# First keys and values by a casting software load, all phi loads from SyncE, and a new order of steps in an attention and expert kernel

## The chip, the cores and the metric

The kernel runs on one core of one Trainium2 chip. The metric is the device time of one execution in microseconds, as the median of repeated runs. The profile beside it shows one execution: the span from the first to the last instruction of the program, and the busy time of the engines in it. The engines are TensorE (PE, with its weight loads as PEld), VectorE (DVE), ScalarE (ACT), GpSimd (POOL) and SyncE (SP). Transfers run on 16 DMA engines; GpSimd issues them on a queue that the profile calls software_dynamic, SyncE and ScalarE on queues called hardware_dynamic.

## The reference

There are 8 batches of 8 heads, 576 positions and a head size of 64. Each head's keys and values are first condensed into 32 memory slots with the weights `softmax(phi)`; the queries then attend to the slots. The result, as 4608 rows of 512, goes through a dense two-layer network and through one of eight experts per row, chosen by the largest gate; the two results are added.

```python
# phi: (8, 8, 576, 32); q, k, v: (8, 8, 576, 64)
a = softmax(phi, axis=2)                      # over the positions
k_m = einsum('bhsm,bhsd->bhmd', a, k)
v_m = einsum('bhsm,bhsd->bhmd', a, v)
x = softmax(q @ k_m.T / sqrt(64)) @ v_m       # then to rows (4608, 512)

y = relu(x @ w1_dense) @ w2_dense
e = argmax(x @ w_gate, axis=1)                # one expert per row
y += softmax(x @ w_gate)[e] * (relu(x @ w1[e]) @ w2[e])
```

(The code above is shortened; the reference is written out with numpy, with small constants added to the sums.)

## The kernel before

The program works on one batch at a time, but the steps of neighbouring batches are interleaved. Every step has a short name and a batch number, and one long text gives the order in which all steps are emitted. Each engine carries out its own instructions strictly in that order, so an instruction that waits holds everything behind it on its engine. A letter behind a step's slash names the engine (A is ScalarE, V VectorE, P GpSimd).

The steps of a batch, in the order of their dependence: `Lphi`, `Lq`, `Lk`, `Lv` load the inputs; `e0`, `e1` take the exponential of phi (ScalarE); `z` and `kv` are the sums and the key-value product (TensorE); `kvm`, `T`, `kTc`, `vTc` scale and transpose it; `q0`, `q1`, `qT0`, `qT1` transpose the queries; `s`, `ET`, `Z`, `ln`, `inv`, `A` are the second softmax; `vg`, `pc`, `choose` find the batch's expert; `w1`, `w2` load that expert's matrices (GpSimd must first read the expert's number); `L`, `mxeq`, `ex`, `gates` are the gates of the rows; `fd`, `vd`, `hd`, `Hd` are the dense hidden layer; `fe`, `ve`, `he`, `He` the expert's; `yd` and `ye` add both second layers into one output bank, chunk by chunk; `Y` copies it to the y tile and `o` stores it.

The order begins so:

```python
ORDER = """
stage3:0 Lq:0 ciota:0 cones:0 stage1:0 Lphi1:0 Lwg:0 wgt:0 Lphi0:0 stage4:0 cast1:0/V cast3:0/P
cid:0 cblk:0 cast4:0/V warm:0/8 stage0:0 stage5:0 warm:0/8 e0:0 warm:0/8 wgm:0 e1:0 wgc:0 cast5:0/A
ciotac:0 cast0:0/P stage2:0 z:0 Lphi:1 q0:0 q1:0 qT0:0/A Lw1d:0 cast2:0/A qT1:0/A kv:0 rz:0 kvm:0
# ... (cut: Lphi:2/A, Lphi:3/A, Lphi:4/A, Lphi:5, Lphi:6/A, Lphi:7 come later, each near its own batch)
```

The loads. The tiles of q, k and v are f16 and the inputs f32, so GpSimd's transfers cast on the way. The exception is batch 0, whose k and v come in six f32 pieces through SyncE and are cast by the engines:

```python
inp = ctx.enter_context(tc.tile_pool(name="inp", bufs=3))      # phi, q, kv: three batches each
big = ...(bufs=2, PSUM); one = ...(bufs=3, PSUM); sml = ...(bufs=1, PSUM)
NKEEP = 4                                                      # y tiles

@step("Lphi")
def _(b, i, e):
    input_tile(b, "phi")
    (nc.scalar if e == "A" else nc.sync).dma_start(
        out=st[b]["phi"].rearrange("p h t m -> p h (t m)"),
        in_=phi[b].rearrange("h (p t) m -> p h (t m)", t=T),
    )

@step("Lv", "Lk")
def _(b, i, e):
    src, u = (v, 1) if i == "Lv" else (k, 0)
    input_tile(b, "kv")
    nc.gpsimd.dma_start(out=st[b]["kv"][:, u]..., in_=src[b]...)   # f32 -> f16
# ... (cut: Lq in the same way; Lphi0 and Lphi1 load the two halves of phi of batch 0)

pieces = [(0, 1, 0, 3, 0), (1, 0, 0, 3, 0), (0, 1, 3, 3, 3), (1, 0, 3, 3, 3), (2, 1, 6, 2, 0), (2, 0, 6, 2, 2)]

@step(*(f"stage{i}" for i in range(len(pieces))))
def _(b, i, e):
    n_tile, u, h0, n, at = pieces[i]
    # ... the stage tiles share the buffers of y:
    # wk.tile([P, 6, T, Dh], F32, tag="y", name="stage", bufs=NKEEP)
    nc.sync.dma_start(out=st[b]["stage", n_tile][:, at : at + n]..., in_=(k, v)[u][b, h0 : h0 + n]...)
```

The output. A chunk of 128 rows leaves PSUM for a y tile, of which there are four, and is stored by SyncE. A fifth batch can write its y only when one of the four has been stored:

```python
@step(*(f"Y{c}" for c in range(NCH)))
def _(b, c, e):
    if "y" not in x:
        x["y"] = wk.tile([128, S * D // 128], F32, tag="y", name="y", bufs=NKEEP)
    # ... ScalarE or VectorE copies p_y to y

@step(*(f"o{c}" for c in range(NCH)))
def _(b, c, e):
    # ... nc.sync.dma_start(out=dst, in_=y[...])
```

Of the kernel before, what the change touches and what calls it, by code (L numbers as in the profile page):

```python
# [24 lines left out]
ex:0 mxeq:0 gates:0 hd3:0 Hd2:0/A hd0:0 Hd3:0/A Lw2d:0 e0:1 pg:0 z:1 rz:1 kv:1 kvm:1 T:1 Hd0:0/A
hd1:0 vTc:1/V vg:1 Hd1:0/A w2:0 fe:0 ve0:0/A vgc:1 ve1:0/V Lq:2 he1:0 Lk:2 pc:1 gB:0/A fd:1 He1:0
kTc:1/A he2:0 He2:0 vd0:1/A Lphi:2/A he0:0 yd2:0 s0:1 He0:0 ET0:1 he3:0 s1:1 yd1:0 He3:0 Z0:1 ET1:1
vd1:1/V Z1:1 ln0:1 ye2:0 inv0:1 ye1:0 ln1:1 Y1:0/V A0:1 yd4:0 ye4:0 inv1:1 yd3:0 q1:2 choose:1 A1:1
Y4:0/A Lv:2 yd0:0 L:1 qT1:2/V e0:2 hd1:1 w1:1 Hd1:1/V ex:1 hd0:1 Hd0:1/A mxeq:1 ye3:0 hd3:1 e1:2
ye0:0 Y0:0/A q0:2 gates:1 Hd3:1/V z:2 Y2:0/A rz:2 kv:2 qT0:2/V hd2:1 kvm:2 pg:1 T:2 Y3:0/A fe:1  # L30
Hd2:1/A gB:1/A w2:1 yd1:1 ve1:1/A vTc:2/V ve0:1/V fd:2 he0:1 vd0:2/A he3:1 Lq:3 vg:2 He0:1 He3:1
vd1:2/A yd4:1 he2:1 Lphi:3/A He2:1 he1:1 kTc:2/A He1:1 yd0:1 s1:2 vgc:2 Lv:3 ye4:1 Lk:3 s0:2 ET1:2
Y4:1/V pc:2 Z1:2 ye0:1 choose:2 ET0:2 ln1:2 Z0:2 Y0:1/V ln0:2 inv1:2 inv0:2 q0:3 w1:2 yd3:1 A1:2
ye1:1 yd2:1 qT0:3/A e0:3 A0:2 L:2 Lq:4 e1:3 mxeq:2 q1:3 hd2:2 ex:2 ye2:1 qT1:3/V Y1:1/A w2:2 gates:2
hd3:2 z:3 Hd2:2/A rz:3 kv:3 Hd3:2/A pg:2 kvm:3 Y2:1/A hd0:2 gB:2/A T:3 Hd0:2/V fe:2 ve1:2/V ye3:1
hd1:2 Lv:4 ve0:2/A he2:2 vTc:3/V Hd1:2/A fd:3 vg:3 He2:2 he0:2 He0:2 vd1:3/A he3:2 Y3:1/A He3:2
yd0:2 Lphi:4/A he1:2 yd3:2 kTc:3/V s0:3 He1:2 vd0:3/V vgc:3 s1:3 ye3:2 ET1:3 Z1:3 ET0:3 ln1:3 Lk:4
pc:3 ye0:2 Y3:2/V inv1:3 Z0:3 yd1:2 q1:4 ln0:3 q0:4 inv0:3 yd2:2 choose:3 A1:3 A0:3 qT1:4/V ye1:2
qT0:4/A hd1:3 e1:4 e0:4 Y0:2/V L:3 mxeq:3 hd2:3 ex:3 yd4:2 gates:3 Y1:2/A w1:3 ye4:2 ye2:2 z:4
Hd2:3/A Hd1:3/A hd3:3 w2:3 o0:2 rz:4 pg:3 Y2:2/A kv:4 Hd3:3/V Y4:2/A Lq:5 fe:3 Lphi:5 kvm:4 gB:3/A  # L40
hd0:3 ve0:3/A Hd0:3/A T:4 ve1:3/V kTc:4/V he3:3 vTc:4/V He3:3 s1:4 ET1:4 vg:4 fd:4 vgc:4 s0:4 pc:4
ET0:4 choose:4 he0:3 he2:3 He0:3 yd2:3 He2:3 e1:5 vd1:4/A he1:3 vd0:4/A Z0:4 yd0:3 ln0:4 Z1:4 He1:3
inv0:4 ln1:4 inv1:4 A0:4 ye0:3 e0:5 ye2:3 q0:5 qT0:5/A Lk:5 q1:5 Y0:3/V yd3:3 Lv:5 A1:4 ye3:3 L:4
yd4:3 ye4:3 Y3:3/A Y4:3/A ex:4 qT1:5/V hd0:4 mxeq:4 gates:4 hd3:4 yd1:3 w1:4 z:5 Hd0:4/A Hd3:4/V
ye1:3 w2:4 Y2:3/A hd2:4 pg:4 gB:4/V fe:4 Y1:3/A rz:5 kv:5 hd1:4 Hd2:4/A ve0:4/A kvm:5 Hd1:4/V T:5
ve1:4/A kTc:5/A vTc:5/A he3:4 he0:4 vg:5 He3:4 fd:5 s0:5 He0:4 vgc:5 yd1:4 vd0:5/V he2:4 vd1:5/A
ET0:5 pc:5 Lq:6 s1:5 yd2:4 He2:4 ET1:5 choose:5 he1:4 He1:4 Lk:6 Z0:5 Lphi:6/A yd0:4 ln0:5 o4:3
inv0:5 Lv:6 Z1:5 ln1:5 o3:2 A0:5 inv1:5 ye1:4 o1:2 q0:6 o2:2 A1:5 qT0:6/V ye2:4 q1:6 qT1:6/A ye0:4
o4:2 Y2:4/V hd0:5 e0:6 e1:6 hd2:5 Y0:4/V L:5 yd3:4 yd4:4 mxeq:5 ex:5 Lphi:7 ye4:4 gates:5 w1:5
Y1:4/A w2:5 z:6 Hd0:5/A kv:6 Hd2:5/A rz:6 Y4:4/V kvm:6 hd1:5 Hd1:5/V pg:5 T:6 kTc:6/A s0:6 gB:5/V  # L50
s1:6 Lq:7 fe:5 ET0:6 vTc:6/V vg:6 ET1:6 ve1:5/V Lv:7 ve0:5/A hd3:5 ye3:4 he2:5 Hd3:5/A vgc:6 he1:5
pc:6 Y3:4/V e0:7 o3:0 He2:5 o2:0 yd2:5 he0:5 He1:5 Z0:6 yd1:5 o4:0 He0:5 ln0:6 he3:5 Z1:6 yd0:5 o0:0
Lk:7 inv0:6 choose:6 He3:5 A0:6 ye0:5 ln1:6 inv1:6 ye1:5 o1:0 ye2:5 A1:6 L:6 q0:7 e1:7 Y0:5/A Y1:5/V
fd:6 q1:7 Y2:5/A yd3:5 vd0:6/V yd4:5 mxeq:6 qT0:7/A vd1:6/A ex:6 hd1:6 gates:6 ye4:5 qT1:7/A w1:6
Hd1:6/A hd2:6 z:7 pg:6 kv:7 Hd2:6/A rz:7 hd3:6 gB:6/A kvm:7 Y4:5/A Hd3:6/V T:7 o4:5 kTc:7/A hd0:6
s1:7 vTc:7/A Hd0:6/A fe:6 o2:3 o3:3 ye3:5 ve1:6/V vg:7 vgc:7 s0:7 ve0:6/A ET1:7 ET0:7 fd:7 o4:1 o0:3
pc:7 he0:6 Y3:5/V vd1:7/A Z1:7 yd0:6 He0:6 o2:1 ln1:7 he2:6 choose:7 He2:6 vd0:7/A inv1:7 he1:6
He1:6 yd1:6 he3:6 o1:3 Z0:7 ln0:7 He3:6 inv0:7 w2:6 yd3:6 A1:7 A0:7 o3:1 ye3:6 ye1:6 o0:5 Y3:6/A
o2:5 Y1:6/A L:7 yd2:6 yd4:6 ye4:6 hd0:7 o4:4 w1:7 hd3:7 Y4:6/V ye2:6 ex:7 o3:5 o1:1 o0:4 Hd0:7/A
hd2:7 Hd3:7/A Y2:6/A mxeq:7 Hd2:7/A o4:6 w2:7 hd1:7 gates:7 fe:7 o1:4 Hd1:7/V ve0:7/V pn:0 o2:4  # L60
# [7 lines left out]
def kernel(  # L68
# [46 lines left out]
    def copy(e, out, in_):  # L115
        (nc.scalar.copy if e == "A" else nc.vector.tensor_copy)(out=out, in_=in_)  # L116
# [78 lines left out]
    pieces = [(0, 1, 0, 3, 0), (1, 0, 0, 3, 0), (0, 1, 3, 3, 3), (1, 0, 3, 3, 3), (2, 1, 6, 2, 0), (2, 0, 6, 2, 2)]

    @step(*(f"stage{i}" for i in range(len(pieces))))
    def _(b, i, e):
        n_tile, u, h0, n, at = pieces[i]
        input_tile(b, "kv")  # L200
        if ("stage", n_tile) not in st[b]:
            st[b]["stage", n_tile] = wk.tile([P, 6, T, Dh], F32, tag="y", name="stage", bufs=NKEEP)
        nc.sync.dma_start(  # L203
            out=st[b]["stage", n_tile][:, at : at + n].rearrange("p h t d -> p h (t d)"),
            in_=(k, v)[u][b, h0 : h0 + n].rearrange("h (p t) d -> p h (t d)", t=T),
        )

    @step(*(f"cast{i}" for i in range(len(pieces))))
    def _(b, i, e):
        n_tile, u, h0, n, at = pieces[i]  # L210
        s = st[b]["stage", n_tile][:, at : at + n]
        o = st[b]["kv"][:, u, h0 : h0 + n]
        if e == "P":
            nc.gpsimd.tensor_copy(out=o, in_=s)
        else:
            copy(e, out=o, in_=s)
# [664 lines left out]
```

## Time and profile before

| what | value |
|---|---|
| time, median of 3 runs | 185.63 us (185.1 to 185.78) |
| span of the profiled execution | 184.1 us |
| PE busy | 150.3 us (82%) |
| DVE busy | 95.0 us (52%) |
| ACT busy | 99.3 us (54%) |
| POOL busy | 33.7 us (18%) |
| moved by the software queue | 22.42 MB, as f16 |
| moved by the two hardware queues | 14.11 and 2.43 MB |

The busy time of an engine is the time in which it had at least one instruction under way. Where the profile says that an engine was idle before an instruction, it also names what released that instruction: another engine's instruction, or a DMA. "Issue" is time in which it waited for nothing that the profile shows. The share of DMA can pass 1, as packets of one DMA engine overlap. In this profile the largest entry among ScalarE's waits is 25.5 us in 5 waits for phi, and in SyncE's most of its time is spent waiting for finished y tiles.

### The profile page before, as it was taken

To read this page: it belongs to the slowest core of one execution; us is meant where nothing else is said; L and a number is where in the kernel's file an instruction comes from. 1 tells how busy PE (TensorE), PEld (TensorE's weight loads), DVE (VectorE), ACT (ScalarE), POOL (GpSimd) and SP (SyncE) were. 2 spreads that over 40 slices of the span, in tenths; PEclk is the share of its full clock that TensorE was granted. 3 is DMA by queue.
4 is the path that set the end of the run, shared out by engine and by line. 5 is a ranking of instruction groups with operands and counts; after the bars stand their busy time and mean duration, and the time that the engine had idled before them with its cause. 6 is when DMAs were issued, how large, how long until landed. Compare 5 with 4: busy or idle time off the path is not lost.

```text
span 184.1 us, 4484 instructions
## 1 busy us (share of the span) xinstructions
PE 150.3 (82%) x1857; PEld 92.6 (50%) x1857; DVE 95.0 (52%) x256; ACT 99.3 (54%) x167; POOL 33.7 (18%) x49
## 2 busy tenths in 40 slices
PE   5015469789999998999964999991889999999990
PEld 5015337445665565566532665561646564565540
DVE  0073029264786565866761467670538546836610
ACT  2023686557384766389717665622473787647030
POOL 2305309000430260017043000340000300300000
PEclk9999999999999999999999999998559999999998
DMA  5999999999999999999999999999995594999994
GB/s 161 214 250 226 191 201 200 205 205 231 185 191 184 232 213 204 206 237 139 227 229 203 206 205 279 240 305 276 212 204 81 78 151 131 330 168 244 390 367 135
DMA packets 40594, 39.30 MB, mean 213 GB/s; under 512 B 1652, under 2 KB 36468, under 8 KB 40568
## 3 DMA queue, kind: packets, MB, share of 16 engines
q0 software_dynamic: 26752, 22.42, 78.1%
q1 hardware_dynamic: 10600, 14.11, 25.7%
q10 hardware_dynamic: 3216, 2.43, 5.0%
q8 instruction: 16, 0.26, 0.5%
q14 instruction: 10, 0.08, 0.1%
HBM read 51.92 MB, written 9.44 MB: 333 GB/s over the span
## 4 chain that ended last, share of the span: by engine, by line
PE 41%; DMA 40%; ACT 9%; SPq 4%; issue 2%; DVE 1%; ACTq 0%
PE p_y L703 18%; DMA out_dram<-y 17%; DMA phi<-in_phi_dram 12%; PE p_h L629 10%; DMA stage<-in_k_dram 7%; DMA w1e<-in_moe_w_dram 4%; PE p_kv L357 3%; PE p_q L413 2%; ACT E L323 2%; PE p_vw L616 2%; PE p_z L456 2%; PE p_s L432 2%; ACT qT L116 1%; SPq L203 1%; ACT lnz L478 1%
## 5 line engine op out<-in xcount | busy, mean ns | idle before, releaser
L703 PE MATMUL p_y<-w2d,HTd 128*128 128x512 f16 (+1 forms) x192 | 37.5, 346 | 4.0 <-ACT vwd L116 3.8
L703 PE MATMUL p_y<-w2e,HTe 128*128 128x512 f16 (+1 forms) x192 | 37.4, 349 | 0.0
L683 DVE SCALAR_TENSOR_TENSOR HTe<-p_h,gB 128x576 f16<-128x576 f32 x32 | 23.3, 753 | 8.9 <-PE p_h L629 5.8
L237 POOL DMA_DIRECT2D w1e<-in_moe_w_dram x8 | 6.1, 761 | 113.8 <-DVE HTe L683 63.9
L323 ACT ACTIVATE E<-phi 96x768 f16<-96x768 f32 x16 | 13.0, 834 | 25.6 <-DMA phi<-in_phi_dram 25.5
L703 PEld LDWEIGHTS <-HTd 128*128 128x128 f16 (+1 forms) x192 | 14.4, 101 | 16.7 <-issue 7.4
L629 PE MATMUL p_h<-A,vwd 128*128 128x288 f16 x128 | 21.9, 307 | 0.4 <-ACT qT L116 0.4
L703 PEld LDWEIGHTS <-HTe 128*128 128x128 f16 (+1 forms) x192 | 15.4, 103 | 13.1 <-issue 1.7
L629 PE MATMUL p_h<-A,vwe 128*128 128x288 f16 x128 | 19.9, 287 | 0.9 <-ACT vwe L116 0.8
L727 ACT ACTIVATE y<-p_y 128x512 f32<-128x512 f32 (+1 forms) x26 | 14.0, 554 | 12.2 <-PE p_y L703 6.4
L670 ACT ACTIVATE HTd<-p_h 128x576 f16<-128x576 f32 x23 | 14.5, 649 | 9.6 <-PE p_h L629 8.1
L483 DVE TENSOR_TENSOR A<-ET,lnz 128x576 f16<-128x576 f16 x16 | 11.9, 753 | 9.7 <-ACT lnz L478 9.7
L445 ACT ACTIVATE ET<-p_s 128x576 f16<-128x576 f32 x16 | 10.1, 651 | 10.3 <-PE p_s L432 10.3
L629 PEld LDWEIGHTS <-vwe 128*128 128x128 f16 x128 | 11.8, 98 | 7.7 <-issue 1.5
L729 DVE TENSOR_SCALAR y<-p_y 128x512 f32<-128x512 f32 (+1 forms) x14 | 8.8, 630 | 13.1 <-PE p_y L703 12.4
L629 PEld LDWEIGHTS <-vwd 128*128 128x128 f16 x128 | 11.9, 103 | 6.5 <-issue 1.2
L469 ACT ACTIVATE lnz<-p_z 128x576 f32<-128x576 f32 x16 | 10.3, 645 | 7.2 <-PE p_z L456 7.1
L413 PE MATMUL p_q<-ident,q 96*128 96x96 f16 x192 | 12.0, 224 | 1.0 <-DMA q<-in_q_dram 1.0
L413 PEld LDWEIGHTS <-q 96*128 96x128 f16 x192 | 10.8, 108 | 3.2 <-DMA q<-in_q_dram 1.6
L478 ACT ACTIVATE lnz<-lnz 128x576 f32<-128x576 f32 x16 | 10.8, 682 | 0.4
L116 ACT COPY qT<-p_q 128x1152 f16<-128x1152 f16 x9 | 10.0, 1115 | 1.7 <-PE p_q L413 1.7
L357 PE MATMUL p_kv<-kv,E 96*32 96x128 f16 x384 | 8.3, 242 | 2.8 <-ACT kv L116 2.3
(88 smaller groups left out, 180.7 us busy)
## 6 DMA issues: line engine op xcount, KB each, us to landing
out_dram<-y SPq DMA_DIRECT2D x32, 256.0 KB, 4.4
q<-in_q_dram POOLq DMA_DIRECT2D x8, 576.0 KB, 13.0
w1e<-in_moe_w_dram POOLq DMA_DIRECT2D x8, 512.0 KB, 7.6
w2e<-in_moe_w_dram POOLq DMA_DIRECT2D x8, 512.0 KB, 11.4
kv<-in_v_dram POOLq DMA_DIRECT2D x7, 576.0 KB, 18.1
kv<-in_k_dram POOLq DMA_DIRECT2D x7, 576.0 KB, 17.9
phi<-in_phi_dram ACTq DMA_DIRECT2D x4, 576.0 KB, 10.9
phi<-in_phi_dram SPq DMA_DIRECT2D x3, 576.0 KB, 13.0
```

What stands on the lines that cost most here:

```text
L116: (nc.scalar.copy if e == "A" else nc.vector.tensor_copy)(out=out, in_=in_)
L323: nc.scalar.activation(out=x["E"][:, :, a].rearrange("p t j m -> p j t m"), in_=x["phi"].rearrange("p (j a) t m -> p a j t m", a=2)[:, a], ...
L357: nc.tensor.matmul(p_kv[M * j : M * j + M, a], lhsT=x["E"][:, t, a, j], rhs=x["kv"][:, :, 2 * j + a, t], start=(t == 0), stop=(t == T - 1),)
L413: nc.tensor.transpose(p_q[:, j // 2, c : c + P], q8[:, 2 * j + a, 2 * t : 2 * t + 2].rearrange("p t d -> p (t d)"), ident,)
L469: nc.scalar.activation(out=st[b]["lnz"][:, a].rearrange("p (h c) -> p h c", h=2), in_=st[b].pop(("pz", a))[:, :, 0:HC], func=AF.Ln,)
L478: nc.scalar.activation(out=lnz, in_=lnz, func=AF.Exp, scale=-1.0)
L483: eng.tensor_mul(out=A[b][:, a], in0=st[b]["ET"][:, a], in1=st[b]["lnz"][:, a])
L629: nc.tensor.matmul(p_h[:, h, 0:HC], lhsT=vw[:, g, 128 * ft : 128 * ft + 128], rhs=a[:, g, HC * h : HC * h + HC], start=(g == 0), stop=(g = ...
L670: nc.scalar.activation(out=o, in_=p_h, func=AF.Relu)
L683: nc.vector.scalar_tensor_tensor(out=x["HTe"][:, ft].rearrange("p (h c) -> p h c", h=2), in0=x.pop(("pe", ft))[:, :, 0:HC], scalar=0.0, in ...
L703: nc.tensor.matmul(p_y[n * u : n * u + n, 0:w], lhsT=HT[:, ft, lo : lo + n], rhs=w2[:, ft, w * u : w * u + w], start=(half == 0 and ft == ...
L727: nc.scalar.activation(out=o, in_=p_y, func=AF.Copy, scale=1.0 / SC)
```

## The change

The f32 pieces and their casts are gone: k and v of batch 0 now come like those of all other batches, by a casting transfer that GpSimd issues. Phi is loaded by SyncE alone. The order of all steps, loads and stores is new; its purpose is to fit the steps to the new start, and to have inputs there when they are due. The work that is computed is the same.

```diff
 ORDER = """
-stage3:0 Lq:0 ciota:0 cones:0 stage1:0 Lphi1:0 Lwg:0 wgt:0 Lphi0:0 stage4:0 cast1:0/V cast3:0/P
-cid:0 cblk:0 cast4:0/V warm:0/8 stage0:0 stage5:0 warm:0/8 e0:0 warm:0/8 wgm:0 e1:0 wgc:0 cast5:0/A
-ciotac:0 cast0:0/P stage2:0 z:0 Lphi:1 q0:0 q1:0 qT0:0/A Lw1d:0 cast2:0/A qT1:0/A kv:0 rz:0 kvm:0
 ... (cut)
+Lv:0 cones:0 Lq:0 cblk:0 Lphi0:0 Lphi:1 e0:0 Lphi1:0 Lk:0 Lwg:0 wgt:0 cid:0 warm:0/8 warm:0/8 Lphi:2
+wgm:0 wgc:0 e0:1 q1:0 e1:0 qT1:0/V z:0 rz:0 kv:0 kvm:0 q0:0 Lw1d:0 T:0 kTc:0/V vTc:0/V s1:0 e1:1
 ... (cut)
-    pieces = [(0, 1, 0, 3, 0), (1, 0, 0, 3, 0), (0, 1, 3, 3, 3), (1, 0, 3, 3, 3), (2, 1, 6, 2, 0), (2, 0, 6, 2, 2)]
-
-    @step(*(f"stage{i}" for i in range(len(pieces))))
-    def _(b, i, e):
 ... (cut: the staging loads)
-    @step(*(f"cast{i}" for i in range(len(pieces))))
-    def _(b, i, e):
 ... (cut: the casts)
```

What the new order makes of the queues:

```text
SyncE:  first half of phi 0, phi 1, second half of phi 0, gate weights, phi 2,
        store o2 of batch 0, phi 4, phi 3, phi 5, phi 6,
        stores o3 of batch 3, o0 of 0, o1 and o2 of 3, o3, o1, o4 of 0, o4 of 2, o0 and o4 of 3,
        phi 7, then the other stores
GpSimd: v0, q0, k0, w1 dense, q1, k1, v1, | w1 of batch 0's expert, w2 dense, q2, w2 of the expert, v2, k2,
        | w1 of batch 1's, q3, w2, k3, v3, | w1 of 2's, q4, w2, v4, k4, | w1 of 3's, w2, k5, q5, k6, v5,
        | w1 of 4's, v6, q6, w2, | w1 of 5's, q7, w2, k7, v7, | w1 and w2 of 6's, | w1 and w2 of 7's
        (a bar is where GpSimd waits to read the number of a chosen expert)
```

More of the change, by code (lines that the diff above doesn't have):

```diff
@@ L19 @@
 ORDER = """
-stage3:0 Lq:0 ciota:0 cones:0 stage1:0 Lphi1:0 Lwg:0 wgt:0 Lphi0:0 stage4:0 cast1:0/V cast3:0/P
-cid:0 cblk:0 cast4:0/V warm:0/8 stage0:0 stage5:0 warm:0/8 e0:0 warm:0/8 wgm:0 e1:0 wgc:0 cast5:0/A
-ciotac:0 cast0:0/P stage2:0 z:0 Lphi:1 q0:0 q1:0 qT0:0/A Lw1d:0 cast2:0/A qT1:0/A kv:0 rz:0 kvm:0
-T:0 kTc:0/A Lq:1 s1:0 ET1:0 Lv:1 s0:0 vTc:0/V vg:0 ET0:0 Z1:0 Z0:0 ln1:0 vgc:0 inv1:0 pc:0 ln0:0
-inv0:0 fd:0 choose:0 e1:1 Lk:1 vd1:0/A q0:1 A0:0 A1:0 q1:1 L:0 vd0:0/V w1:0 qT0:1/A qT1:1/V hd2:0
@@ L25 @@
[L25 to L60, printed above, removed]
@@ L61 @@
-ve1:7/A pg:7 ye0:6 gB:7/A he2:7 He2:7 Y0:6/A he0:7 He0:7 yd2:7 he1:7 he3:7 o0:1 He1:7 yd0:7 o1:6
-o1:5 yd3:7 He3:7 ye2:7 flags:0 o0:6 o2:6 o3:6 Y2:7/A ye3:7 yd1:7 Y3:7/A ye1:7 o2:7 Y1:7/V ye0:7
-Y0:7/A o3:7 yd4:7 o3:4 ye4:7 o1:7 Y4:7/A o0:7 o4:7/A
+Lv:0 cones:0 Lq:0 cblk:0 Lphi0:0 Lphi:1 e0:0 Lphi1:0 Lk:0 Lwg:0 wgt:0 cid:0 warm:0/8 warm:0/8 Lphi:2
+wgm:0 wgc:0 e0:1 q1:0 e1:0 qT1:0/V z:0 rz:0 kv:0 kvm:0 q0:0 Lw1d:0 T:0 kTc:0/V vTc:0/V s1:0 e1:1
+vg:0 qT0:0/A ET1:0 s0:0 Z1:0 ciota:0 vgc:0 ET0:0 ciotac:0 Lq:1 ln1:0 pc:0 choose:0 inv1:0 Z0:0 fd:0
@@ new lines @@
+ln0:0 q1:1 Lk:1 A1:0 vd1:0/A inv0:0 Lv:1 vd0:0/V q0:1 w1:0 qT0:1/A A0:0 qT1:1/V L:0 mxeq:0 ex:0
+hd0:0 hd3:0 Hd3:0/A z:1 hd1:0 rz:1 kv:1 gates:0 kvm:1 Hd0:0/A Lw2d:0 hd2:0 Hd1:0/A T:1 Hd2:0/V e0:2
+pg:0 kTc:1/V gB:0/A fe:0 vTc:1/A ve0:0/A s0:1 vg:1 ve1:0/V s1:1 vgc:1 ET0:1 Lq:2 fd:1 w2:0 ET1:1
+pc:1 he3:0 he1:0 yd0:0 He3:0 e1:2 He1:0 vd0:1/V Z1:1 vd1:1/A he0:0 yd2:0 He0:0 choose:1 he2:0 ln1:1
+He2:0 yd3:0 Z0:1 q1:2 qT1:2/V inv1:1 ye2:0 ln0:1 ye3:0 Lv:2 inv0:1 Y2:0/A A1:1 yd4:0 q0:2 A0:1 o2:0
+L:1 mxeq:1 hd0:1 Lphi:4 ye4:0 qT0:2/A ex:1 Y3:0/A ye0:0 z:2 Y4:0/A rz:2 Lphi:3 yd1:0 Lk:2 hd2:1
@@ new lines @@
+gates:1 kv:2 Hd0:1/A Hd2:1/A hd1:1 w1:1 hd3:1 kvm:2 T:2 ye1:0 Hd3:1/V Y0:0/V kTc:2/A vTc:2/A pg:1
+Hd1:1/A vg:2 s1:2 gB:1/V fe:1 ET1:2 ve0:1/V ve1:1/A s0:2 vgc:2 Y1:0/V ET0:2 Lq:3 pc:2 he0:1 e1:4
+fd:2 He0:1 he3:1 He3:1 yd2:1 w2:1 vd1:2/A vd0:2/A Z1:2 ln1:2 he2:1 yd3:1 He2:1 Z0:2 he1:1 He1:1
+ln0:2 inv1:2 yd0:1 A1:2 inv0:2 q0:3 ye0:1 A0:2 choose:2 ye2:1 Y2:1/V qT0:3/A q1:3 Y0:1/V Lk:3 L:2
+qT1:3/A ye3:1 yd1:1 hd3:2 hd1:2 Lphi:5 mxeq:2 ex:2 yd4:1 Hd3:2/A e1:3 e0:3 ye4:1 ye1:1 Y3:1/V
+Hd1:2/V Lv:3 gates:2 hd0:2 w1:2 hd2:2 z:3 Hd2:2/A kv:3 rz:3 kvm:3 pg:2 Y4:1/A Lq:4 T:3 w2:2 Y1:1/A
@@ new lines @@
+Hd0:2/A gB:2/V fe:2 kTc:3/A ve0:2/A ve1:2/V s0:3 Lphi:6 s1:3 ET1:3 yd1:2 vTc:3/A he0:2 fd:3 ET0:3
+Lv:4 vd1:3/A vg:3 He0:2 vgc:3 he3:2 Z1:3 ln1:3 He3:2 vd0:3/A pc:3 yd3:2 Lk:4 he2:2 he1:2 e0:4 yd0:2
+inv1:3 He2:2 q0:4 He1:2 Z0:3 ye3:2 choose:3 ln0:3 ye0:2 q1:4 w1:3 A1:3 inv0:3 w2:3 Y0:2/A ye1:2 A0:3
+yd4:2 qT1:4/V qT0:4/A Y3:2/V Y1:2/A L:3 hd1:3 ex:3 yd2:2 mxeq:3 hd0:3 e1:6 ye2:2 gates:3 Hd1:3/A z:4
+kv:4 Hd0:3/V hd3:3 pg:3 rz:4 Y2:2/A kvm:4 Hd3:3/V fe:3 ye4:2 gB:3/A ve0:3/A T:4 Y4:2/A hd2:3 Lk:5
@@ new lines @@
+ve1:3/V he1:3 kTc:4/V vTc:4/V vg:4 fd:4 Hd2:3/A s0:4 He1:3 vd1:4/A vgc:4 yd4:3 vd0:4/V ET0:4 e0:5
+he3:3 He3:3 yd2:3 he2:3 pc:4 he0:3 He2:3 yd1:3 He0:3 Z0:4 ye4:3 e1:5 Lq:5 s1:4 ln0:4 ET1:4 Lk:6
+ye2:3 choose:4 Z1:4 inv0:4 ye1:3 Y4:3/V Y2:3/V A0:4 ln1:4 q0:5 inv1:4 q1:5 A1:4 yd0:3 Y1:3/A qT1:5/V
+Lv:5 L:4 mxeq:4 ye0:3 w1:4 hd1:4 e0:6 ex:4 yd3:3 Lv:6 qT0:5/A gates:4 z:5 Hd1:4/V kv:5 pg:4 rz:5
+Y0:3/A gB:4/A kvm:5 hd0:4 T:5 fe:4 Hd0:4/V kTc:5/A vTc:5/V s1:5 ve1:4/V s0:5 ye3:3 ET1:5 ve0:4/V
+Z1:5 vg:5 ET0:5 ln1:5 hd2:4 vgc:5 Hd2:4/A Y3:3/A inv1:5 hd3:4 fd:5 o3:3 Hd3:4/V he0:4 Lq:6 pc:5
@@ new lines @@
+He0:4 Z0:5 kv:6 ln0:5 w2:4 vd0:5/A he2:4 vd1:5/A he3:4 yd0:4 A1:5 He2:4 he1:4 o0:0 yd1:4 He3:4 o1:3
+o2:3 inv0:5 A0:5 He1:4 L:5 choose:5 mxeq:5 o3:0 q1:6 ye1:4 ex:5 q0:6 z:6 rz:6 ye0:4 w1:5 kvm:6
+qT0:6/A T:6 yd4:4 ye4:4 o1:0 qT1:6/A o4:0 kTc:6/V Y1:4/V s0:6 Y0:4/V gates:5 s1:6 ET1:6 yd2:4 Y4:4/V
+yd3:4 hd3:5 o4:2 ET0:6 hd2:5 Hd3:5/A Hd2:5/A ye2:4 vTc:6/V Z1:6 hd1:5 ln1:6 inv1:6 vg:6 Lq:7 Y2:4/V
+Hd1:5/V o0:3 vgc:6 fe:5 ve1:5/A hd0:5 o4:3 ve0:5/V Z0:6 pc:6 ln0:6 ye3:4 Hd0:5/V inv0:6 w2:5 pg:5
+he2:5 Lk:7 yd3:5 Lphi:7 A1:6 gB:5/A Y3:4/A e0:7 He2:5 e1:7 he0:5 he1:5 yd0:5 A0:6 L:6 He0:5 He1:5
@@ new lines @@
+he3:5 He3:5 ex:6 Lv:7 choose:6 yd1:5 q0:7 q1:7 ye3:5 ye1:5 mxeq:6 ye0:5 z:7 Y1:5/A qT1:7/V gates:6
+Y3:5/A pg:6 Y0:5/V fd:6 gB:6/A yd2:5 ye2:5 w1:6 vd0:6/A rz:7 vd1:6/V qT0:7/A hd2:6 o0:5 hd0:6 Y2:5/A
+kv:7 yd4:5 Hd0:6/A w2:6 Hd2:6/V kvm:7 ye4:5 T:7 Y4:5/A o1:2 fe:6 o0:2 vTc:7/V hd3:6 hd1:6 ve1:6/V
+ve0:6/A o2:2 Hd3:6/A fd:7 Hd1:6/V vg:7 vgc:7 he3:6 vd0:7/A He3:6 he1:6 He1:6 yd3:6 o2:1 he0:6 he2:6
+o4:4 o0:4 kTc:7/A vd1:7/A He0:6 pc:7 yd4:6 choose:7 s0:7 yd0:6 w1:7 ET0:7 He2:6 s1:7 o3:2 ye4:6 o3:5
@@ new lines @@
+Z0:7 o4:5 ET1:7 ye0:6 ln0:7 inv0:7 Y4:6/V Z1:7 ln1:7 Y0:6/V yd2:6 A0:7 w2:7 inv1:7 ye2:6 A1:7 yd1:6
+Y2:6/V L:7 hd3:7 ex:7 hd0:7 ye3:6 o2:5 mxeq:7 Hd3:7/A Hd0:7/A o0:1 o2:6 Y3:6/A hd2:7 Hd2:7/A hd1:7
+o3:4 gates:7 Hd1:7/V fe:7 pn:0 pg:7 ve1:7/A ye1:6 ve0:7/V he1:7 gB:7/A o4:6 He1:7 he3:7 o3:1 yd1:7
+o4:1 He3:7 o3:6 o1:1 Y1:6/A he2:7 o1:5 he0:7 o1:6 He2:7 yd3:7 He0:7 o1:4 yd0:7 ye3:7 Y3:7/V ye1:7
+ye0:7 yd2:7 o0:6 Y0:7/V o3:7 o2:4 Y1:7/A ye2:7 o1:7 yd4:7 ye4:7 Y2:7/A Y4:7/A o0:7 o2:7 flags:0
+o4:7/A
@@ L193, in _ @@
         )
-    pieces = [(0, 1, 0, 3, 0), (1, 0, 0, 3, 0), (0, 1, 3, 3, 3), (1, 0, 3, 3, 3), (2, 1, 6, 2, 0), (2, 0, 6, 2, 2)]
-    @step(*(f"stage{i}" for i in range(len(pieces))))
-    def _(b, i, e):
[L199 to L206, printed above, removed]
-    @step(*(f"cast{i}" for i in range(len(pieces))))
-    def _(b, i, e):
[L210 to L216, printed above, removed]
     @step("Lw1d")
```

## The prediction

> **What bounds the kernel now.** I began with the page's slices, because they show which engine is full when.
>
> ```profile
> ## 2 busy tenths in 40 slices
> PE   5015469789999998999964999991889999999990
> ...
> ACT  2023686557384766389717665622473787647030
> ...
> PEclk9999999999999999999999999998559999999998
> DMA  5999999999999999999999999999995594999994
> ```
>
> One slice is 4.6 us. The DMA row is full from the second slice to 138 us: until then transfers never rest. TensorE is full except in the first 40 us and in two dips near 97 and 127 us, and after the second dip its granted clock is at half. So neither engine alone is the bound: TensorE runs at full rate wherever it has data, and the question is where it waits. Next, the same in stretches cut at the dips (columns: stretch, its length, busy us and count of PE, PEld, DVE, ACT, POOL, granted clock, DMA share, GB/s):
>
> ```profile
> 20.00:40.00 20.00, 15.24 (x244) 10.30 (x243) 9.19 (x29) 12.82 (x22) 4.79 (x7) 1.00 1.27 202
> ...
> 95.00:99.00 4.00, 0.24 (x2) 0.05 (x1) 0.76 (x1) 1.35 (x3) 3.30 (x5) 1.00 1.30 210
> 99.00:124.50 25.50, 25.49 (x307) 15.87 (x308) 15.60 (x38) 15.04 (x26) 3.83 (x5) 1.00 1.23 244
> 124.50:129.50 5.00, 0.42 (x8) 0.25 (x5) 0.00 (x0) 1.67 (x4) 0.00 (x0) 0.83 1.17 270
> 129.50:138.00 8.50, 7.96 (x112) 4.88 (x112) 4.20 (x14) 4.97 (x9) 0.00 (x0) 0.50 1.30 207
> ```
>
> Two holes of about 3.8 and 4.6 us, then 8.5 us of work at half clock. What ends the holes is in ScalarE's timeline (start, length, instruction, in brackets the idle time before it and what ended it):
>
> ```profile
> 97.65 0.84 ACT L323 ACTIVATE E<-phi 96x768 f16<-96x768 f32 x1 [4.71 <-DMA phi<-in_phi_dram]
> ```
> ```profile
> 127.83 1.57 ACT L323 ACTIVATE E<-phi 96x768 f16<-96x768 f32 x2 [5.73 <-DMA phi<-in_phi_dram]
> ```
>
> Both are waits for a phi tile, with ScalarE stuck in its order and TensorE behind it. The phi of the first was issued only at 84.65 us, behind an output store on SyncE, and took 12.98 us; that of the second was issued at 115.46 us by ScalarE among 13 stores and took 12.3 us. The start is last: the chain of waits there is
>
> ```profile
> 4.54 12.69 DMA stage<-in_k_dram
> ...
> 17.98 1.11 ACT qT L116
> 19.09 1.11 ACT kv L116
> 20.20 0.04 issue
> 20.24 1.48 PE p_kv L357 x43
> ```
>
> The f32 pieces land by 19.0 us, ScalarE casts the last after another copy, and the first key-value product starts at 20.24 us.
>
> How fast the queues move is in the DMA view of 20 to 40 us, where the software queue is nearly alone, and of 60 to 64 us, where a phi shares the engines (packets, MB, share):
>
> ```profile
> q0 software_dynamic: 4643, 3.99, 125.8%
> ```
> ```profile
> q0 software_dynamic: 662, 0.50, 79.5%
> q10 hardware_dynamic: 559, 0.43, 42.6%
> ```
>
> Alone the software queue writes 3.99 MB / 20 us = 0.20 MB/us of f16. A q, k or v of 0.59 MB costs 2.95 us, an expert matrix of 0.52 MB 2.6 us. Beside a phi it makes 0.50 MB in 4 us instead of 0.80, so 0.43 MB of phi take 0.30 MB from it; a phi of 0.59 MB costs it 0.41 MB, or 2.1 us. In 112 to 116 us, beside stores, it made 0.36 MB while 0.78 MB were stored.
>
> [...]
>
> **The change part by part.**
>
> *Staging.* Removed are six f32 loads (2.36 MB) and six casts: two on GpSimd of 1.14 us, two on VectorE (0.98, 0.56), two on ScalarE (0.83, 1.15). Only the last, and the 1.11 us copy ahead of it, lies on the path. Added are two software loads of 0.59 MB. DMA time is nearly unchanged: in 12.5 to 15.5 us staging alone ran at 237 GB/s, so 2.36 MB are 10 us; two software loads are 5.9 us. But three phi tiles (0, 1, 2) now stand beside v0, q0, k0, where before there were two. All six are 3.54 MB; at the shared rate of (0.50 + 0.43) / 4 = 0.23 MB/us that is 15.4 us. From a first packet near 2 us, plus an allowance of 2 us for the last of the queue, k0 lands at 17.5 to 20, and I choose 19.5. The product then starts at once: 20.24 - 19.5 = 0.7 us gained. The casts that leave ScalarE did not hold anything else.
>
> *Phi early.* In the new order phi 1 and 2 go out at the start, phi 4, 3 and 5 right after one early store (o2 of batch 0), phi 6 when a buffer comes free. Without the two waits TensorE's holes close: 3.8 + 4.6 = 8.4 us. Without the second hole the half clock goes too: 7.96 us of work at half rate would have taken 4.0.
>
> *Order.* TensorE's work stays: 144.2 us busy from 20 to 184 us, less the 4 of the half clock, is 17.5 us a batch. The software queue needs per batch 3 x 2.95 + 2 x 2.6 = 14.1 us, with a phi 16.2. So loads keep ahead of TensorE as long as stores stay out, and those are kept back in four y buffers until batch 4, as before. The half clock of the first 32 us (46 products took 1.47 us at 20 us, 48 took 0.85 at 34) should stay[...].
>
> Sum without new waits: 184.1 - 0.7 - 8.4 - 4.0 = 171.0 us span.
>
> *New waits, estimated from the same rates.* To say when a step comes, I added the TensorE work ahead of it in the new order, by the pieces in the chain of waits of before (0.86 us for half a y chunk, 0.53 for a hidden block or half of q, 0.79 for the key-value product), and to that the 19.5 us of the start and 8.7 us that the start loses to short dependent steps at half clock: before, 52.69 - 20.24 = 32.45 us lay between the products of batches 0 and 2, with 23.8 us of work in them. Phi 4 is issued after Y2 of batch 0 (17.4 us of work, so about 45 us), behind a store; phis took 9 to 13 us, so it lands at 55 to 58. Its exponential has 27.9 us of work ahead, 56 us: 2 us of wait. All of batch 0's stores must land before the first y of batch 4. SyncE holds them behind a store that waits for a y of batch 3 (80.6 us of work, 110 us with a little loss), and they are then 1.70 MB; at 0.195 MB/us (0.78 / 4) plus 2 us they land at 121 or later. The y stands at 91.9 us of work, 121: 1.5 us. Phi 7 stands behind ten stores and lands near 131; its exponential is due at 130: 1 us. The expert matrices, k and v of batches 2 to 6 have only 1 to 4 us in hand, since GpSimd's queue stops at each choice of an expert: 2 us over all. Together 6.5 us: 177.5 us span. The median time stands 1.5 us above the span (185.63 against 184.1), so 179.0 us.
>
> **The rivals.**
>
> *The loads take over.* If the software queue is the true bound, closing the phi holes only moves the wait to w1e or to keys and values, and nothing comes of it but the start. For it: DMA is full to 138 us, and GpSimd once let the queue run dry (issue at 82.29 us, previous landing at 84.97, next at 88.24 instead of 87.6). Against it: TensorE waited 0.2 us for w1e in the whole run and 0.5 for k. This gives 182 to 186 us.
>
> [...]If the stores before batch 4 or phi 7 come several us late, the clock halves again: 5 us of hole and 4 of half clock. For it: ScalarE already waited 5.2 us once for a store to free y. Against it: TensorE can go on with three output banks in hand. This gives 184 to 188 us.
>
> *A slower start.* If phi 1 and 2 really go before k0, all starts 2 to 3 us later than before; but these loads are then out of the way later. This gives 180 to 183 us.
>
> *Everything fits.* If the new waits are absorbed, about 171 + 1.5 = 172.5, the floor; end-of-kernel stores make 174 more likely.
>
> **Range and chances.** Most of the gain rests on two holes that one cause explains, and I think it 70% likely that at least 4 us of the 12.4 remain, which is a gain over 2% (under 181.9 us). The range from the fitting order to a single new hole at its cheap end is 174 to 185. Within 2%: 0.22, for the rival of the loads. Slower by over 2% (above 189.3 us) needs two new holes: 0.08.
>
> **What would show it.** The phi step is right if ScalarE's waits for phi after the start fall from 10.4 us in two to under 4, and if the granted clock shows no half after 40 us. The start is right if the first key-value product comes at 18 to 20 us, waiting for k by DMA. The queue step is right if software loads land 15.5 to 17 us a batch with no landing gap over 4 us. It is wrong if TensorE has a hole over 3 us between 40 and 165 us whose releaser is w1e, w2e, kv or a store; then the named rival has taken the gain. If TensorE's busy time differs by more than 4 us from 146, the work itself has changed its speed, which I don't expect.

## The result and the profile after

The changed kernel takes 176.52 us (median of 4 runs, 174.72 to 177.58); the kernel before took 185.7 us beside it. The ratio is 0.9475, with a 95% interval of 0.9397 to 0.9553. The span of the profiled execution fell from 184.1 to 174.4 us. A second comparison (e12 below) gave 0.9439 (0.9348 to 0.953).

The page's slices of the changed kernel, the same rows as before; a slice is now 4.4 us:

```profile
PE   4012687989998899899999998998999989999960
...
ACT  3330087585635864885765947825754843764120
...
PEclk9999999699999999999999999999999999999995
DMA  5999999999999999999999999999999999899882
```

The two dips of TensorE are gone, and so is the half clock in the middle of the run. After the start only one slice, at about 31 us, is below full clock, beside the last one, where nothing is left to do. The clock row says nothing of the start: the trace holds no clock record before 27.48 us (32.19 us in the kernel before), and the row shows that as full. The products tell more: the first 48 of the key-value sums took 1.47 us, the same 48 of batch 3 took 0.85 us; in the kernel before, 48 of them took 0.85 us at a granted 1.00 (at 33.93 us) and 1.47 at 0.50 (at 130.03). The DMA row stays full until the stores at the end.

The start, in TensorE's timeline (start, length, instruction, and the idle time before it with what ended it):

```profile
19.43 1.47 PE L333 MATMUL p_kv<-kv,E 96*32 96x128 f16 x48 [1.49 <-DMA kv<-in_k_dram]
31.92 1.36 PE L333 MATMUL p_kv<-kv,E 96*32 96x128 f16 x44
```

The first key-value product now waits for a load alone, and starts 0.8 us earlier than before.

Where did the 9.7 us of span come from? TensorE's own gaps give most of it. Added up from the trace, all gaps after 21 us, short ones too, are 15.0 us before and 7.5 us now. The earlier start gives 0.8. The tail, from TensorE's last instruction to the end, takes some back: 4.7 us before (179.46 to 184.1), 5.9 us now (168.53 to 174.4). What is left, 9.7 - 7.5 - 0.8 + 1.2 = 2.6 us, is work that ran faster; the largest stretch of that kind is the 10.24 us at half clock.

Which waits were they? The view of TensorE's waits between 40 and 168 us says it (columns: who waited for whom, us in total, times, the longest), first of the kernel before:

```profile
PE p_att L335 <- ACT ex L569: 4.9, 2, 4.6
PE p_y L703 <- ACT vwd L116: 3.8, 1, 3.8
...
PE p_kv L357 <- DMA kv<-in_k_dram: 0.5, 1, 0.5
...
PE p_vw L616 <- DMA w1e<-in_moe_w_dram: 0.2, 1, 0.2
```

and of the changed kernel:

```profile
PE p_vw L592 <- DMA w1e<-in_moe_w_dram: 1.0, 2, 0.5
PE p_att L355 <- DVE kvm L344: 0.9, 2, 0.7
PE p_y L679 <- DMA w2e<-in_moe_w_dram: 0.7, 2, 0.4
PE p_y L679 <- DVE y L705: 0.7, 1, 0.7
```

The two large entries name ScalarE; ScalarE stood behind phi in both. They have gone. Waits for expert matrices have come in their place, but they are small: 1.7 us in four.

### The profile page after: what moved, and what is told of

It reads as the page before. It is cut to its first block, busy times and chain, and to the rows that moved or that the text cites. A ratio compares the mean times of both kernels' runs of the same rounds, so it can differ in the third digit from the quotient of the medians.

```text
span 174.4 us, 4447 instructions
## 1 busy us (share of the span) xinstructions
PE 145.7 (84%) x1849; PEld 89.9 (52%) x1849; DVE 99.0 (57%) x263; ACT 93.1 (53%) x156; POOL 33.1 (19%) x49
## 4 chain that ended last, share of the span: by engine, by line
PE 48%; DMA 37%; ACT 4%; issue 3%; DVE 3%; POOL 2%; POOLq 1%; ACTq 0%
PE p_y L679 23%; DMA w2e<-in_moe_w_dram 18%; PE p_h L605 13%; DMA kv<-in_k_dram 9%; DMA w1e<-in_moe_w_dram 9%; PE p_kv L333 3%; PE p_vw L592 2%; PE p_q L389 2%; PE p_z L432 1%; ACT lnz L445 1%; POOL q L189 1%; PE p_s L408 1%; PE p_g L572 1%; PE p_att L522 1%; ACT lnz L454 1%
## 5 line engine op out<-in xcount | busy, mean ns | idle before, releaser
L679 PE MATMUL p_y<-w2e,HTe 128*128 128x512 f16 (+1 forms) x192 | 36.5, 345 | 0.7 <-DMA w2e<-in_moe_w_dram 0.7
L679 PEld LDWEIGHTS <-HTd 128*128 128x128 f16 (+1 forms) x192 | 14.9, 101 | 13.8 <-issue 3.9
L679 PEld LDWEIGHTS <-HTe 128*128 128x128 f16 (+1 forms) x192 | 14.7, 101 | 13.2 <-issue 1.7
L605 PE MATMUL p_h<-A,vwd 128*128 128x288 f16 x128 | 20.4, 296 | 0.5 <-ACT HTd L646 0.5
L115 ACT COPY qT<-p_q 128x1152 f16<-128x1152 f16 x10 | 11.1, 1120 | 14.3 <-PE p_q L389 14.3
L703 ACT ACTIVATE y<-p_y 128x512 f32<-128x512 f32 (+1 forms) x22 | 11.8, 552 | 12.4 <-PE p_y L679 12.2
L299 ACT ACTIVATE E<-phi 96x768 f16<-96x768 f32 x16 | 13.0, 837 | 10.1 <-DMA phi<-in_phi_dram 10.1
L646 ACT ACTIVATE HTd<-p_h 128x576 f16<-128x576 f32 x19 | 12.0, 651 | 9.0 <-PE p_y L679 5.4
L705 DVE TENSOR_SCALAR y<-p_y 128x512 f32<-128x512 f32 (+1 forms) x18 | 11.4, 644 | 8.3 <-PE p_y L679 4.2
L648 DVE TENSOR_SCALAR HTd<-p_h 128x576 f16<-128x576 f32 x13 | 9.8, 756 | 9.6 <-PE p_y L679 5.5
L445 ACT ACTIVATE lnz<-p_z 128x576 f32<-128x576 f32 x16 | 10.4, 648 | 7.3 <-PE p_z L432 7.1
L421 ACT ACTIVATE ET<-p_s 128x576 f16<-128x576 f32 x16 | 10.1, 658 | 5.4 <-PE p_s L408 5.3
```

Of the source, the lines that this page charges most:

```text
L299: nc.scalar.activation(out=x["E"][:, :, a].rearrange("p t j m -> p j t m"), in_=x["phi"].rearrange("p (j a) t m -> p a j t m", a=2)[:, a], ...
L445: nc.scalar.activation(out=st[b]["lnz"][:, a].rearrange("p (h c) -> p h c", h=2), in_=st[b].pop(("pz", a))[:, :, 0:HC], func=AF.Ln,)
L605: nc.tensor.matmul(p_h[:, h, 0:HC], lhsT=vw[:, g, 128 * ft : 128 * ft + 128], rhs=a[:, g, HC * h : HC * h + HC], start=(g == 0), stop=(g = ...
L646: nc.scalar.activation(out=o, in_=p_h, func=AF.Relu)
L679: nc.tensor.matmul(p_y[n * u : n * u + n, 0:w], lhsT=HT[:, ft, lo : lo + n], rhs=w2[:, ft, w * u : w * u + w], start=(half == 0 and ft == ...
L703: nc.scalar.activation(out=o, in_=p_y, func=AF.Copy, scale=1.0 / SC)
```

## The experiments

All ratios are to the kernel before, run beside each experiment on the same chip. I stated three theories. A: the late phi loads made both holes and the half clock, and that is most of the gain. B: the software loads are the bound, and take over any wait that is removed. C: the rest of the new order of steps counts.

| run | what it is | median us | ratio | 95% interval |
|---|---|---|---|---|
| e1 | before, all phi early | 181.76 | 0.9665 | 0.9567 to 0.9763 |
| e9 | before, phi 5 and 6 early | 183.65 | 0.9654 | 0.9523 to 0.9784 |
| e3 | before, no staging | 185.05 | none | |
| e8 | before, all phi early, no staging | 181.63 | 0.9588 | 0.9495 to 0.9682 |
| e10 | before, phi 5 and 6 early, no staging | 180.68 | 0.9631 | 0.9541 to 0.972 |
| e4 | before, second hole filled | 183.73 | 0.9791 | 0.9697 to 0.9886 |
| e2 | changed, phi late | 179.8 | 0.9675 | 0.9612 to 0.9738 |
| e5 | changed, phi from ScalarE | 176.65 | 0.9479 | 0.9398 to 0.9561 |
| e6 | changed, w2 loaded once | 174.89 | 0.9433 | 0.9352 to 0.9514 |
| e7 | changed, phi 1 and 2 after k0 | 177.32 | 0.9544 | 0.947 to 0.9617 |
| e11 | changed, warm start | 175.45 | 0.9323 | 0.9224 to 0.9421 |
| e12 | changed, again | 176.94 | 0.9439 | 0.9348 to 0.953 |

The time before was 188.18 us beside e1, e3, e4 and e8, 186.4 us beside e2, e5, e6 and e7, and 188.69 us beside e9 to e12, so medians of different groups are not to be set against each other. The medians are of all executions, while the ratios leave out those more than 1.5% above the fastest of their kernel: e3 kept only one of four and so has no ratio, and the profiles of e3, e8 and e9 are of such longer executions.

### All phi early in the old order (e1)

```diff
- ... Lphi:1 ... Lphi:2/A ... Lphi:3/A ... Lphi:4/A ... Lphi:5 ... Lphi:6/A ... Lphi:7 ...
+ ... Lphi:1 Lphi:2 Lphi:3 ... (Lphi:b right after the exponentials of batch b-3, for b = 4 to 7) ...
```

> The kernel before, with nothing changed but the loads of phi 2 to 7: all from SyncE, each as soon as its buffer is free (before, two of them were issued at 84.65 and 115.46 us and ended the two holes of TensorE). Staging, casts and the order of all other steps stay. Theory A (late phi made both holes and the half clock after the second): both holes close, and the time falls from 185.7 to 174-178 us, most of the change's gain of 9.2 us. Theory B (the software loads are the bound, the phi waits only stand in front of them): the wait moves to w1e, k or v and the time stays at 182-186 us. Theory C (the new order of the compute steps is what counts): 181-184 us.

Measured 0.9665, which is 6.3 us less of 188.2. Both holes closed (no gap of TensorE after 40 us is longer than 1.3 us) and no half clock came after 40 us. But the ratio, 179.5 us when set to a time before of 185.7, lies between what A and what C had said, and the profile shows what was paid for it, at the start (TensorE's timeline of this run):

```profile
28.87 0.63 PE L614 MATMUL p_vw<-w1d,vT 64*32 64x512 f16 x8 [3.34 <-DMA w1d<-in_moe_w_dense_dram]
31.77 2.10 PE L411 MATMUL p_q<-ident,q 96*128 96x96 f16 x24 [2.28 <-DMA q<-in_q_dram]
...
37.81 0.85 PE L355 MATMUL p_kv<-kv,E 96*32 96x128 f16 x48
```

Phi 2 and 3, which nobody needs yet, took the DMA engines from w1d and q of batch 1. From 15 to 32 us the software queue moved 1.42 MB where it had moved 2.44 in the kernel before, and SyncE's queue 2.22 MB where it had moved 0.99. That makes 5.6 us of waits, and the second product starts at 37.81 us instead of 33.93. Early was good here only as far as it did not stand in front of what was due.

### Only the two late phis (e9), and without staging (e10)

```diff
- ... yd0:2 Lphi:4/A he1:2 ... fe:3 Lphi:5 kvm:4 ... Z0:5 Lphi:6/A yd0:4 ...
+ ... yd0:2 Lphi:4/A Lphi:5 Lphi:6 he1:2 ... fe:3 kvm:4 ... Z0:5 yd0:4 ...
# SyncE has no other work there and issues each when its buffer is free; e10 has e3's edit too
```

> The kernel before with only phi 5 and phi 6, the two whose late issue ended the holes, moved: SyncE issues each as soon as its buffer is free (about 50 and 70 us instead of 84.65 and 115.46). The start stays as it was. The run with all phis early gave 0.9665 of the time before, with both holes closed but 4 us lost at the start, where phi 2 and 3 took the engines from w1d and q of batch 1. Theory A (the two holes and the half clock are most of the gain): 0.945 to 0.965 of the time before, no gap of TensorE over 1.5 us after 40 us, no half clock there, second key-value product at 34 us as before. If the loads only pass the wait on: 0.975 or more.

> The same, and v, q, k of batch 0 by software load without staging. Left to the changed kernel is then the rest of the new order. If staging is worth its 0.7 us at the start: the same as the kernel with the two phis moved, within 1%, and within 1% of the changed kernel (0.9475). If the rest of the new order carries a part of its own: 0.96 or more.

The second product came at 34.07 us in e9, so the start is whole again. The ratio, 0.9654, lies just above A's range, and its interval is wide. The rest of A's forecast failed in the profiled execution (185.68 us, the longest of the four): TensorE had gaps of 1.7 and 1.9 us, both waits for keys or values, all its waits for software loads between 40 and 168 us came to 6.1 us, and the clock did halve, at 131.5 us, after the gap of 1.9 us.

e10 gave 0.9631, which is e9's ratio within 1%, but A wanted 0.9475 within 1%. The changed kernel, e12 in the same group, gave 0.9439; the two intervals do not overlap. So the rest of the new order carries a part of its own, about 2%. TensorE's waits between 40 and 168 us in e10 tell what it is:

```profile
PE p_vw L613 <- DMA w1e<-in_moe_w_dram: 3.0, 3, 1.3
PE p_kv L354 <- DMA kv<-in_v_dram: 1.2, 1, 1.2
PE p_q L410 <- DMA q<-in_q_dram: 1.2, 1, 1.2
PE p_kv L354 <- ACT y L724: 1.0, 1, 1.0
PE p_y L700 <- DMA w2e<-in_moe_w_dram: 0.5, 1, 0.5
```

and in e12, the changed kernel:

```profile
PE p_att L355 <- DVE kvm L344: 0.9, 2, 0.7
PE p_vw L592 <- DMA w1e<-in_moe_w_dram: 0.6, 2, 0.4
```

With the phi holes closed, the old order waits 5.9 us for software loads (3.0 + 1.2 + 1.2 + 0.5), where the kernel before waited 0.7. That is theory B, at work in the old order. The new order meets the same loads with 0.6 to 1.7 us of waits (e12 and the first profile). TensorE's last instruction ends at 171.9 us in e10 and at 166.9 in e12, and its gaps between 40 and 168 us are 8.0 and 3.1 us, so the waits account for nearly all of the difference. The new order moves loads, stores and compute steps at once; which of these does it was not separated.

### All phi early and no staging (e8), no staging alone (e3)

```diff
-stage3:0 Lq:0 ... stage1:0 ... stage4:0 cast1:0/V cast3:0/P ... cast2:0/A ... kv:0
+Lv:0 Lq:0 Lk:0 ... kv:0                          # e3; e8 has e1's phi edit too
```

> Both of the above edits on the kernel before: phi early from SyncE and no staging; only the order of the other steps is still the old one. What then is missing to the changed kernel (176.5 us) is the worth of the rest of the new order. Theory A: 173.5-177.5 us, so the rest is worth 0 to 1 us or less than nothing. Theory C: 180 us or more.

> The kernel before, with v, q, k of batch 0 by the casting software load as in the changed kernel, and the six f32 pieces and their casts gone; phi and the order of all other steps as before. Theory A: only the start moves, 0.5 to 1.5 us, the holes stay: 184-186 us. Rival (the casts and the f32 traffic held more than the start): 181 us or less.

e8 gave 0.9588, between A and C, and its interval overlaps that of the changed kernel; by itself it decides nothing. In e3 one of four executions took 181.53 us and the other three 185.03 to 185.23. Against 188.18 us that is 3 us at least, more than the 0.5 to 1.5 that I expected, but one group without a ratio does not settle it. The profiles say more about the start: in e3 the first product came at 19.73 us and the second at 33.43 (before: 20.24 and 33.93), and in e10 the second came at 31.97, against 34.07 in e9. So the start without staging is worth 0.5 to 2 us by the second product. In e3's profile the first hole was also shorter, 1.5 us instead of 3.8, and the half clock after the second hole lasted 3.4 us instead of 10.24. Whether the missing staging did that, or the one execution, was not settled.

### The half clock alone (e4)

```diff
+    @step("hot")                      # 56 products into unused columns of an output bank
+    def _(b, i, e):
+        for _ in range(int(e)):
+            nc.tensor.matmul(st[b]["p_y", 4][:, 256:384], lhsT=onesb, rhs=onesb, start=True, stop=True)
- ... w1:5 Y1:4/A w2:5 z:6 ...
+ ... w1:5 Y1:4/A w2:5 hot:4/56 z:6 ...
```

> The kernel before with 56 idle 128x128 products put in front of the sums of batch 6 (they write unused columns of an output bank, nothing reads them): they run in the second hole of 4.6 us and leave less than 2 us of it idle. The hole itself stays. If the half clock after the hole costs what I worked out (4 us), the granted clock shows no 0.5 there and the time is 181-182.5 us; if the loads or other engines set the pace in those 10 us, the clock stays full and the time is 184.5-186 us.

Measured 0.9791: 3.9 us of 188.2, with an interval from 2.1 to 5.7 us. Set to a time before of 185.7 that is 181.8 us, inside the first forecast. The stretches of the profile around both holes (columns as in the prediction; the third number from the right is the granted clock):

```profile
90.00:98.00 8.00, 4.18 (x51) 2.25 (x49) 3.95 (x11) 2.33 (x5) 3.84 (x5) 1.00 1.25 222
98.00:103.00 5.00, 4.60 (x16) 1.94 (x16) 1.69 (x3) 4.12 (x7) 0.00 (x0) 0.66 1.29 204
124.00:131.00 7.00, 5.85 (x109) 4.91 (x109) 1.43 (x9) 2.40 (x5) 0.00 (x0) 1.00 1.22 234
131.00:140.00 9.00, 8.34 (x130) 5.35 (x119) 6.96 (x20) 5.46 (x10) 0.00 (x0) 1.00 1.18 182
```

Behind the filled hole the granted clock is 1.00 up to 140 us, where it was 0.50 from 127.76 us before. (Behind the first hole, which was left as it was, it fell for 3.4 us in this execution; before it had not.) Between the products of batches 6 and 7 lie 18.1 us here and 21.1 us before, so the half clock was worth 3 us there. A wait that could not be removed thus cost less here when it was filled with work that nobody reads.

### Late phi in the new order (e2), phi from ScalarE (e5)

```diff
- ... Lphi:4 ... Lphi:3 ... Lphi:5 ... Lphi:6 ...                  # early, SyncE
+ ... Y4:0/A Lphi:4/A ... ln0:2 Lphi:3/A ... e0:4 Lphi:6/A ... e1:6 Lphi:5/A ...   # e2
+ ... Lphi:4/A ... Lphi:3/A ... Lphi:5/A ... Lphi:6/A ...          # e5: the changed kernel's own places
```

> The changed kernel with phi 3 to 6 issued late again, by ScalarE, about 8 us before each is due, as the two that made the holes were; all else as changed. Theory A (when phi is issued is what counts): each lands 9 to 13 us after its issue, so waits of 2 to 5 us come back, 4 of them; 181-188 us. Rival (the new order has room for it): 176-178.5 us.

> The changed kernel with phi 3 to 6 issued by ScalarE instead of SyncE at the same places of the order; they still go out at least 8 us ahead of their use, phi 5 some 20 us later than from SyncE. If only the moment counts and not the engine: 175.5-178 us (4 issues of 0.32 us on ScalarE). If SyncE as such brought something: 179 us or more.

e2 gave 0.9675 against the 0.9475 of the change: 2%, or 3.7 us, come back. That is less than A said (181 us or more at 186.4 before; measured 179.8) and more than the rival's 176 to 178.5. ScalarE's waits for phi rose only a little, from 10.1 us in five to 12.7 in seven, the longest 2.9; no gap of TensorE after 40 us was over 1.7 us, and no half clock came there. The new order can bear a late phi better than the old one could. e5 is 0.9479 against 0.9475: who issues phi was worth nothing that could be measured here; when it is issued was worth the 2% of e2.

### What sets the pace now (e6)

```diff
-        st[b]["w2"] = expert_w2(st[b]["ev"])
+        st[b]["w2"] = expert_w2(st[b]["ev"]) if b == 0 else st[0]["w2"]
```

> The changed kernel with the second expert matrix loaded for batch 0 only and used for all batches: 7 loads of 0.52 MB, 18 us of the software queue, are left out, and the result is that of another expert. If the loads set the pace of the changed kernel (each key-value product starts within 0 to 1.5 us of its last load): 165-171 us. If TensorE sets it and the loads only keep up: it can win no more than its idle gaps after 40 us (about 4 us) and 0 to 1 us at the end: 172-175.5 us.

Seven loads, 18 us of the software queue, are left out, and the ratio is 0.9433 against 0.9475: 0.8 us, which the intervals don't tell from nothing. TensorE's wait for w1e fell to 0.2 us, that for w2 is gone, and its gaps between 40 and 168 us fell from 4.9 us (3.1 in e12) to 2.1. The last keys or values of batch 7 landed at 132.4 us instead of 138.4, but their product started at 136.7 instead of 139.5: it stood 4.3 us behind its load, where it had stood 1.1 us behind. So after the start TensorE sets the pace of the changed kernel; the loads keep up, though in the changed kernel each key-value product starts within 2 us of its last load's landing.

The changed kernel's page could mislead here. Its chain of work that ended last gives, as shares of the span:

```profile
PE 48%; DMA 37%; ACT 4%; issue 3%; DVE 3%; POOL 2%; POOLq 1%; ACTq 0%
```

Half of the 37% is put down to w2, and leaving out seven of the eight loads of w2 was worth 0.8 us.

### The start (e7, e11)

```diff
-... Lphi0:0 Lphi:1 e0:0 Lphi1:0 ... Lphi:2 wgm:0 wgc:0 e0:1 q1:0 e1:0 qT1:0/V z:0 ...
+... Lphi0:0 e0:0 Lphi1:0 ... wgm:0 wgc:0 q1:0 e1:0 qT1:0/A Lphi:1/A Lphi:2/A z:0 ... inv0:0 e0:1 e1:1   # e7
+... wgm:0 warm:0/40 wgc:0 e0:1 q1:0 e1:0 qT1:0/V z:0 warm:0/12 ...                                  # e11
```

> The changed kernel with phi 1 and 2 kept out of the way of v0, q0, k0: ScalarE issues them after its first copy of the queries, and the exponentials of batch 1 stand later in its order. k0 should land near 14-16 us instead of 19.4 and the first key-value product start there. If the loads of the first 31 us are one sum (v1 lands at 30-31 us in both orders), little of the 4-5 us is left at the second product: 175-177 us. If the dependent steps of the start are what counts: 172-173 us.

> The changed kernel with 52 more idle 128x128 products while TensorE waits for q0 and k0 (40 after the gate weights' products, 12 after the sums of batch 0), so that its clock is full at the first key-value product and not from 27 us. The work from 19.4 to 34 us then runs at full clock: 48 products of the key-value sums in 0.85 instead of 1.47 us. If that work is on the path: 1 to 2.5 us less than the changed kernel. If the loads of the first 31 us hold the second product anyway (v1 lands at 30.7): 0 to 0.7 us.

In e7 the first product starts 3 us earlier, but the second where it was (TensorE's timeline):

```profile
16.41 1.47 PE L331 MATMUL p_kv<-kv,E 96*32 96x128 f16 x48 [1.44 <-DMA kv<-in_k_dram]
24.71 2.10 PE L387 MATMUL p_q<-ident,q 96*128 96x96 f16 x24 [1.82 <-DMA q<-in_q_dram]
31.89 1.36 PE L331 MATMUL p_kv<-kv,E 96*32 96x128 f16 x44 [1.68 <-DMA kv<-in_v_dram]
```

New waits, for q (1.82 us) and for v of batch 1 (1.68), ate what was won, and the ratio is 0.9544, no better than the change. So the order of the loads changed who waited, and not when the second product came: 31.89 us here, 31.92 in the changed kernel. In e11 the first product takes 0.85 us instead of 1.47, which is what it takes at a granted 1.00, and the second starts at 31.15 us. The clock fell to half at 25.4 us, for 10.24 us, and the second product took 1.47 us again. The ratio is 0.9323 against 0.9439 of the change beside it: the lowest of all, and 1.5 us less by the medians, but the intervals overlap, so the gain is likely and not shown.

## Why the prediction was right, point by point

*The start.* I chose 19.5 us for the first product; it came at 19.43. In e12 the same kernel's came at 18.45, so the range of 17.5 to 20 was right and the hit within it luck. I had taken one shared rate of 0.23 MB/us for all the loads of the start; from 2 to 19.43 us the DMA engines moved 3.87 MB, which is 0.22. The gain by the second product was larger than 0.7, namely 2.0 us (33.93 to 31.92).

*The phi holes.* Both closed. ScalarE's waits for phi after the start fell to 4.2 us in two, just over the 4 that I had named. Before, they were not 10.4 us in two but 14.9 in four: I had left out two of 3.0 and 1.4 us, at 49.5 and 66.9 us. The causal weight is smaller than the sum made it look: in the old order closing the holes brought 3.4% of 5.3% (e1, e9), because waits for software loads moved in: between 40 and 168 us 4.0 us of them in e1, 6.1 in e9 and 5.9 in e10, against 0.7 before. In the new order, taking early phi away costs 2% (e2).

*The half clock.* Predicted 4.0 us; the remainder of TensorE's account is 2.6 us, and e4 put it at 3.9 us of time and 3 us within the profile. That the second hole brought the half clock is shown (0.50 behind it, 1.00 once it was filled), and its size is somewhat less than I said. That any hole of several us would halve the clock, as the rival of a new hole has it, was my assumption and was not shown: the first hole, 3.8 us long, cost no clock. The last section has what was measured around the holes.

*New waits.* This is the term that was mis-sized: 6.5 us predicted. The waits themselves came about where I had placed them: ScalarE waited 1.88 us for phi 4 (predicted 2) and 2.28 us for phi 7 (1), and y tiles waited for stores, VectorE 0.8 us before batch 4's first y (1.5). But TensorE's gaps over 0.25 us between 40 and 168 us add up to 4.4 us in all, and the kernel before had 1.2 us of such gaps beside its two holes. So the new waits cost TensorE about 3.2 us, half of my term. Its waits for expert matrices were 1.7 us, close to the 2 predicted for loads; phi 4 cost it 0.6 us, the stores 0.7 and phi 7 nothing over 0.25. I had added waits of ScalarE and of stores to the span as if TensorE had no other work in front of it.

*The sum.* The span came out 3.1 us shorter than 177.5. The new waits alone would explain 3.3 us, but other terms were off as well: up to 40 us the change gained 2.8 us where I had said 0.7 (0.8 by the earlier start, 2.0 because TensorE's gaps from 21 to 40 us fell from 4.5 to 2.6 us), the half clock gave 1.4 us less by TensorE's account, and the tail lost 1.2 us. That these three nearly cancel is luck.

*The queue.* My sign for this step failed: software loads were to land 15.5 to 17 us a batch, with no gap over 4 us between landings. The first expert matrices of neighbouring batches landed 13.9 to 20.4 us apart, and seven gaps between landings after 40 us are over 4 us. The longest, 9.8 us, lies between 115.20 and 124.97 us: the load that ends it was issued only at 117.14 us, with nothing left on the queue before it, and from 109.9 us on stores were issued. I had also taken all of the 0.78 MB of 112 to 116 us for stores, though SyncE had issued a phi on the same queue at 112.76 us. Even so TensorE's waits for software loads stayed at 1.7 us. An even flow was not needed.

*The rivals.* The loads taking over is what the old order does with early phi, and what the new order mostly avoids (e10 against e12); I had given it to the change as a whole. A new hole did not come. A slower start did not come to the change, but did to e1 by its second product.

*The tail* grew by 1.2 us, which I had left out. In both kernels the last stores are issued 0.45 us after TensorE's end. The last one landed 3.1 us later before and 3.6 us later now, and from there to the end of the program it was 1.1 and 1.8 us. The cause was not followed up.
